# A transformer block on one core: the last second products go row tile by row tile, and a group's norm is spread over more tiles

## The chip, the cores and the metric

The kernel runs on one core of a Trainium2 chip. A core has engines that run beside each other, each through its own list of instructions in order: TensorE (PE in the profile; PEld is its loading of the stationary operand), VectorE (DVE), ScalarE (ACT) and GpSimd (POOL). SyncE (SP) issues the DMA transfers. An instruction that needs another engine's result waits on a semaphore, and everything behind it on its own engine waits with it. The metric is the time of one execution on the device, in microseconds (us); the median of several executions is compared.

## The reference

```python
h = _layernorm(x) * (1 + ca) + sa
x = x + ga * _A_ref(h, A_wqkv, A_wo)      # 16 heads, causal window of 256
h = _layernorm(x) * (1 + cb) + sb
x = x + gb * _B_ref(h, B_w1, B_b1, B_w2)

def _B_ref(x, w1, b1, w2):
    h = x @ w1 + b1
    act = h * tanh(softplus(h))            # Mish
    return act @ w2
```

There are 2048 rows of 448 float32 values; the feed-forward part `_B_ref` goes from 448 to 1792 columns and back. The six vectors sa, ca, ga, sb, cb, gb come from `silu(c) @ w_mod`. The change lies in the second half, the feed-forward part.

## The kernel before

**Precision.** Float32 products are made of two reduced-precision halves: a tensor is split into a high part and what is left, and a product is the sum of high by high, high by low and low by high. So `w13` and `w1l` are the two halves of the first weights, `w2h` and `w2l` those of the second, `hh` and `hl` those of the normalised input and `ah` and `al` those of the activation.

**Tiling.** The 2048 rows are four groups of 512 (`NG`, `GT`), and the 1792 hidden columns are 14 tiles of 128 (`NF`). The feed-forward part is one loop over n from 0 to 56 (`NN` is 56): n stands for group n // 14 and hidden tile n % 14. Attention fills the span up to about 370 us; the loop takes the rest.

**One step of the loop** (lines 1227 to 1246) issues, in this order:

- `f1_mm(n)`: the first product, 11 matmuls into one PSUM bank `z`. There are two such banks.
- `f1_act(n)`: ACT's Mish from `z` to `t`, ACT's copy to `ah`, and DVE's subtraction that gives `al` (lines 976 to 978). There are two buffers each of `ah` and `al`, one of `t`.
- `pieces(n)`, in the first group alone: the split of the weights that are still missing. Per tile this puts one copy `w2h` on ACT and one subtraction `w2l` on POOL.
- one `fill_step()`.
- `ff2(n - 1)`: the second product of the tile before, 12 matmuls: for each of the four row tiles t, three matmuls (`ah` by `w2h`, `ah` by `w2l`, `al` by `w2h`) into the bank `acc[g][t]`. On the last hidden tile of a group the row tile is finished: it is multiplied by `gbn` and the residual `x1` is added, in a buffer `yo` of which there are three (tag "xr"), and SP stores it.
- more `fill_step()`s: three in the first group, two in the others.

The order that is written here is the order on each engine; nothing rearranges it.

**What the fill steps do.** `fill` is a generator that hands out work beside the loop, a piece at each step. In the first group it first finishes the attention output of the last row group (`gen_oT`, `gen_wo`), and then makes the second group's normalised input: `gen_x1_ln2(1)`, which is `gen_ln2`. That is four DVE passes `xn` (one per row tile of 128), for which `XN2[g]` is set when they start, and then `ln2_blocks`: for each of four column chunks ci, 16 DVE transposes of 32x128 (four in one step, line 897), and then the two stages that `pipe` starts on its later steps: `hi(ci)`, which is ACT's `hhf` and behind it, in place, DVE's `yt` (lines 882 and 883), and `lo(ci)`, which is POOL's `hlf` (line 887). The third and fourth groups' inputs are made in the same way in groups 1 and 2, from their third tile on.

**The last group's finish.** For g = 3 the residual is added by POOL for row tiles 0 to 2, and for row tile 3 in two halves, 256 columns on DVE and 192 on POOL:

```python
for eng, a, b in (((DVE, 0, D),) if g < NG - 1 else ((POOL, 0, D),) if t < 3 else
                  ((DVE, 0, 256), (POOL, 256, D))):
    eng.tensor_tensor(y[:, a:b], y[:, a:b], x1[g][:, t, a:b], op=ALU.add)
```

Of the kernel before, what the change touches and what calls it, by code (L numbers as in the profile page):

```python
# [9 lines left out]
F32R = mybir.dt.float32r  # L10
BF16 = mybir.dt.bfloat16
AF = mybir.ActivationFunctionType
ALU = mybir.AluOpType

S, D, F, H, DH, W = 2048, 448, 1792, 16, 28, 256
NG, GT = 4, 512
# [35 lines left out]
def adaln_block(ctx: ExitStack, tc: tile.TileContext, x, wqkv, wo, w1, b1, w2, c, w_mod, out):  # L52
    nc = tc.nc
    PE, ACT, DVE, POOL = nc.tensor, nc.scalar, nc.vector, nc.gpsimd
# [3 lines left out]
    def dma(o, i):  # L58
        nc.sync.dma_start(o, i)

    def pool(name, side="left", space=None):
        kw = {} if space is None else {"space": space}
        cm = tc.tile_pool(name=name, bufs=1, reuse_waits="tile", side=side, **kw)
        st = ExitStack()
        return st.enter_context(cm), st
# [19 lines left out]
    def bank(tag, bufs, name):  # L85
        return PS[0].tile([128, 512], F32, name=name, tag=tag, bufs=bufs)
# [461 lines left out]
    def xr_tile(name):  # L548
        return mid.tile([128, 512], F32, name=name, tag="xr", bufs=3)
# [252 lines left out]
    FW = {}  # L802
    w2h, w2l, w2p, h2, x1 = {}, {}, {}, {}, {}
# [100 lines left out]
    XN2 = {}  # L904
# [37 lines left out]
    def pieces(f):  # L942
        for i, (kind, n) in enumerate(SEQ):
            if kind == "w2" and n == f:
                w2_split(n)
            elif kind == "w1" and (n - 4) // 2 == f:
                w1_hi(n)
                w1_lo(n, DVE if f < 1 else POOL)
            else:
                continue  # L950
            if "ff" in FW:
                piece_load(i + 6)

    NN = NG * NF
    ah, al, acc = {}, {}, {}

    def ftile(nm, n, dt=F32):
        return FW["p1"].tile([128, GT], dt, name=f"{nm}{n}", tag=nm, bufs=1 if nm == "t" else 2)
# [3 lines left out]
    def f1_mm(n, tag, part=(0, 11)):  # L962
        g, f = divmod(n, NF)
        hh, hl = h2[g]
        fs = slice(f * 128, (f + 1) * 128)
        if part[0] == 0:
            zb[n] = bank(tag, 2, f"z{n}")
        ps = passes(hh, hl, FW["w13"][:, :, fs], FW["w1l"][:, :, fs])
        for m in range(*part):
            PE.matmul(zb[n], ps[m][1], ps[m][0], start=(m == 0), stop=(m == 10))  # L970

    def f1_act(n):
        f = n % NF
        ah[n], al[n] = ftile("ah", n, F32R), ftile("al", n, F32R)
        t = ftile("t", n)
        ACT.activation(t, zb[n], AF.Mish, bias=FW["b1c"][:, f:f + 1])  # L976
        ACT.activation(ah[n], t, AF.Copy)  # L977
        DVE.tensor_tensor(al[n], t, ah[n].bitcast(F32), op=ALU.subtract)  # L978

    def mish_table():  # L980
# [4 lines left out]
    TAIL = {  # L985
        0: lambda: (f1_mm(0, "mm", (0, 6)), pieces(0)),
        1: lambda: (f1_mm(0, "mm", (6, 11)), mish_table(), f1_act(0)),
        2: lambda: f1_mm(1, "mm", (0, 6)),
        3: lambda: (f1_mm(1, "mm", (6, 11)), f1_act(1)),
    }  # L990

# [132 lines left out]
    for u in range(NU + 7):  # L1124
        s, k = divmod(u, 3)
        g = s // H
# [19 lines left out]
        if g < NG:  # L1146
# [6 lines left out]
            n = 0  # L1153
# [26 lines left out]
    ff, ff_s = pool("ff")  # L1180
    FW["ff"] = ff
    p1, gbn = FW["p1"], FW["gbn"]

    def ff2(n):
        g, f = divmod(n, NF)
        if f == 0:
            acc[g] = [bank("acc", 4, f"acc{g}_{t}") for t in range(4)]
        for t in range(4):
            ts = slice(t * 128, (t + 1) * 128)
            p = acc[g][t][:, 0:D]  # L1190
            PE.matmul(p, ah[n][:, ts], w2h[f], start=(f == 0), stop=False)  # L1191
            PE.matmul(p, ah[n][:, ts], w2l[f], start=False, stop=False)  # L1192
            PE.matmul(p, al[n][:, ts], w2h[f], start=False, stop=(f == NF - 1))  # L1193
            if f == NF - 1:
                j = 4 * g + t
                y = xr_tile(f"yo{j}")[:, 0:D]
                DVE.tensor_tensor(y, p, gbn, op=ALU.mult)
                for eng, a, b in (((DVE, 0, D),) if g < NG - 1 else ((POOL, 0, D),) if t < 3 else
                                  ((DVE, 0, 256), (POOL, 256, D))):
                    eng.tensor_tensor(y[:, a:b], y[:, a:b], x1[g][:, t, a:b], op=ALU.add)  # L1200
                dma(of[j * 128:(j + 1) * 128, :], y)

    def gen_x1_ln2(g):
        if g > 1:
            x1_load(g, (ff, p1)[g % 2])
            yield
            yield
            yield

        def xn_tiles():  # L1210
            t = XN2[g] = mid.tile([128, 4, 512], F32, name=f"xn2_{g}", tag="on", bufs=2)
            return [t[:, i] for i in range(4)]
        yield from gen_ln2(g, ff, xn_tiles, "tr", 2)
# [8 lines left out]
    def fill_step():  # L1222
        if fill is not None:
            pipe.step()
            next(fill, None)
            flush()
    for n in range(NN + 1):
        g, f = divmod(n, NF)
        if f == 0 and n:
            while fill is not None and next(fill, "END") != "END":  # L1230
                pipe.step()
            fill = None
            while pipe.items:
                pipe.step()
        if f == 2 and 0 < g < NG - 1:
            fill = gen_x1_ln2(g + 1)
        if 2 <= n < NN:
            f1_mm(n, "z")
            f1_act(n)
        if 0 < n < NF:  # L1240
            pieces(n)
        if n:
            fill_step()
            ff2(n - 1)
            for _ in range(2 + (g == 0)):
                fill_step()
    for st in (ff_s, mid_s, cst_s, FW["s"], psf_s):
        st.close()
# [23 lines left out]
```

## Time and profile before

| what | us |
|---|---|
| median of the 3 runs shown (661.86 to 669.27) | 663.73 |
| the profiled execution, its own time | 668.01 |
| its span, first to last instruction | 666.2 |
| the feed-forward loop within it, from the first second product on | 371.3 to 659.6 |

The profiled execution is 4.28 us above the median. The profile lists, for each engine, how long it was busy and what it waited for; in the timeline a row has the start, the duration, the engine, the source line and the tile, and in brackets how long the engine sat idle before it and which instruction ended that idle time. Matmuls overlap: a matmul is listed with 0.36 to 0.40 us, but one starts every 0.20 us (448 columns) or 0.23 us (512 columns) when nothing is missing.

### The profile page before, as it was taken

To read this page: it belongs to the slowest core of one execution; us is meant where nothing else is said; L and a number is where in the kernel's file an instruction comes from. 1 tells how busy PE (TensorE), PEld (TensorE's weight loads), DVE (VectorE), ACT (ScalarE), POOL (GpSimd) and SP (SyncE) were. 2 spreads that over 40 slices of the span, in tenths; PEclk is the share of its full clock that TensorE was granted. 3 is DMA by queue.
4 is the path that set the end of the run, shared out by engine and by line. 5 is a ranking of instruction groups with operands and counts; after the bars stand their busy time and mean duration, and the time that the engine had idled before them with its cause. 6 is when DMAs were issued, how large, how long until landed. Compare 5 with 4: busy or idle time off the path is not lost.

```text
span 666.2 us, 10727 instructions
## 1 busy us (share of the span) xinstructions
PE 634.8 (95%) x3712; PEld 514.3 (77%) x3712; DVE 391.1 (59%) x1138; ACT 335.6 (50%) x584; POOL 120.6 (18%) x173
## 2 busy tenths in 40 slices
PE   3998999999999999999988999999999999999996
PEld 3786777677887678877756898878888888888885
DVE  5765686675678767578777334954584438631112
ACT  4544567588875778635668633432233224323221
POOL 6652000043011200000030445340021001100002
PEclk9997999599999999999999999999999999999999
DMA  8786676547754478435852853003000300010001
GB/s 215 211 233 215 225 245 213 147 114 227 270 172 142 141 224 307 147 110 151 235 150 69 261 148 106 11 1 111 0 1 0 112 1 0 1 55 1 1 0 55
DMA packets 49169, 83.77 MB, mean 126 GB/s; under 512 B 5838, under 2 KB 27612, under 8 KB 49116
## 3 DMA queue, kind: packets, MB, share of 16 engines
q1 hardware_dynamic: 49116, 83.10, 40.6%
q8 instruction: 29, 0.48, 0.3%
q14 instruction: 24, 0.20, 0.1%
HBM read 53.45 MB, written 29.36 MB: 124 GB/s over the span
## 4 chain that ended last, share of the span: by engine, by line
PE 74%; issue 11%; DVE 8%; DMA 3%; ACT 2%; SPq 1%; POOL 1%; POOLq 0%; DVEq 0%; ACTq 0%
PE z L970 15%; PE qk L321 10%; PE pv L769 7%; PE sA L687 6%; PE sB L731 6%; PE wo L321 5%; PE acc L1193 4%; PE acc L1191 4%; PE acc L1192 4%; PE qk_v L321 4%; DVE yt L897 3%; DMA k<-scr 2%; PE sB L759 2%; DVE junk L689 1%; PE qk L506 1%
## 5 line engine op out<-in xcount | busy, mean ns | idle before, releaser
L689 DVE CUSTOM_DVE_ANT_0 junk<-sA,strip 128x384 bf16<-128x384 f32 (+2 forms) x256 | 135.4, 529 | 80.6 <-PE sA L687 65.8
L734 ACT ACTIVATE P<-sB 128x512 f32<-128x512 f32 (+2 forms) x192 | 108.3, 570 | 84.5 <-PE sB L731 82.1
L978 DVE TENSOR_TENSOR al<-t,ah 128x512 fp32r<-128x512 f32 x56 | 41.2, 735 | 137.2 <-ACT ah L977 136.9
L976 ACT ACTIVATE t<-z,b1c 128x512 f32<-128x512 f32 x56 | 38.4, 686 | 156.8 <-PE z L970 145.0
L970 PE MATMUL z<-hhf,w 128*128 128x512 f32 x224 | 88.9, 397 | 0.0
L970 PE MATMUL z<-hlf,w 128*128 128x512 f32 x224 | 88.8, 397 | 0.0
L731 PE MATMUL sB<-q,k 86*128 86x384 f32 (+1 forms) x352 | 87.2, 323 | 0.7 <-ACT sB L739 0.7
L687 PE MATMUL sA<-k,q 84*128 84x384 f32 (+2 forms) x256 | 82.4, 360 | 4.3 <-DMA k<-scr 2.7
L1193 PE MATMUL acc<-w2h,al 128*128 128x448 f32 x224 | 82.1, 366 | 1.9 <-DVE al L978 1.9
L1191 PE MATMUL acc<-w2h,ah 128*128 128x448 f32 x224 | 81.9, 366 | 0.0
L1192 PE MATMUL acc<-w2l,ah 128*128 128x448 f32 x224 | 81.8, 365 | 0.0
L731 PEld LDWEIGHTS sB<-q,k 86*128 86x128 f32 x352 | 60.3, 197 | 11.1 <-ACT sB L739 4.4
L970 PE MATMUL z<-hhf,w1l 128*128 128x512 f32 x168 | 66.5, 396 | 0.0
L897 DVE STREAM_TRANSPOSE yt<-xn 32x128 f32<-32x128 f32 x192 | 58.1, 302 | 2.6
L687 PEld LDWEIGHTS sA<-k,q 84*128 84x128 f32 x256 | 48.4, 197 | 10.4 <-DVE mx L689 2.7
L739 ACT ACTIVATE sB<-strip 128x512 f32<-128x512 bf16 (+2 forms) x95 | 54.6, 575 | 3.0
L769 PE MATMUL pv<-P,v 128*32 128x256 f32 (+2 forms) x704 | 50.2, 399 | 0.4 <-DVE on L790 0.4
L970 PEld LDWEIGHTS z<-hlf,w 128*128 128x128 f32 x224 | 42.1, 188 | 10.1
L970 PEld LDWEIGHTS z<-hhf,w 128*128 128x128 f32 x224 | 42.1, 188 | 9.1 <-issue 0.6
L1193 PEld LDWEIGHTS acc<-w2h,al 128*128 128x128 f32 x224 | 42.1, 188 | 5.9 <-DVE al L978 2.6
L1191 PEld LDWEIGHTS acc<-w2h,ah 128*128 128x128 f32 x224 | 42.1, 188 | 5.0
L1192 PEld LDWEIGHTS acc<-w2l,ah 128*128 128x128 f32 x224 | 42.1, 188 | 4.7
(155 smaller groups left out, 1029.1 us busy)
## 6 DMA issues: line engine op xcount, KB each, us to landing
k<-scr SPq DMA_DIRECT2D x48, 252.0 KB
q<-scr SPq DMA_DIRECT2D x64, 168.0 KB
scr<-st SPq DMA_DIRECT2D x21, 512.0 KB
scr<-st SPq DMA_DIRECT2D x29, 256.0 KB
x<-x1d SPq DMA_DIRECT2D x10, 448.0 KB
xin<-in_A_x_dram SPq DMA_DIRECT2D x8, 448.0 KB
xr<-in_A_x_dram SPq DMA_DIRECT2D x16, 224.0 KB
x1d<-xr SPq DMA_DIRECT2D x16, 224.0 KB
```

Of the source, the lines that this page charges most:

```text
L321: PE.matmul(p, b, a, start=(n == 0), stop=(n == 10))
L687: PE.matmul(p[:, c0:384], q[0:84, t * 128:(t + 1) * 128], k[0:84, t * 128 + c0:t * 128 + 384], start=True, stop=True)
L689: DVE.tensor_tensor_reduce(out=junk[:, c0:384], in0=p[:, c0:384], in1=mask[:, c0:384], scale=1.0, scalar=-3.0e38, op0=ALU.add, op1=ALU.max ...
L731: PE.matmul(p[:, c:c + 128 * (t1 - t0)], k[:, jj * 128:(jj + 1) * 128], q[:, t0 * 128:t1 * 128], start=False, stop=True, skip_group_check= ...
L734: ACT.activation(P[:, c0:], p[:, c0:], AF.Exp, scale=SCALE)
L739: ACT.activation(p[:, c0:], strip[:, c + c0:c + 512], AF.Copy)
L769: PE.matmul(pvb[q][32 * a:32 * a + 32, t0 * 128:t1 * 128], V[j % NV][:, h + a, :], Pt[4 * w + a][:, c:c + 128 * (t1 - t0)], start=(b == 0 ...
L897: DVE.transpose(y4[32 * j:32 * j + 32, ci, :, 32 * i:32 * i + 32], x4[32 * i:32 * i + 32, :, ci, 32 * j:32 * j + 32])
L970: PE.matmul(zb[n], ps[m][1], ps[m][0], start=(m == 0), stop=(m == 10))
L1191: PE.matmul(p, ah[n][:, ts], w2h[f], start=(f == 0), stop=False)
L1192: PE.matmul(p, ah[n][:, ts], w2l[f], start=False, stop=False)
L1193: PE.matmul(p, al[n][:, ts], w2h[f], start=False, stop=(f == NF - 1))
```

## The change

Three things change, in the functions `f1_act` and `ff2` and in the loop.

1. The second products of the last three tiles (n = 53, 54, 55) are no longer issued a step behind their first products. They all go to the end, behind the first product of tile 55: first row tiles 0 and 1 of tile 53; then, for each row tile in turn, what it still lacks (54 and 55 for row tiles 0 and 1; 53, 54 and 55 for 2 and 3). Since three activations are then alive at once, tile 55 gets buffers for `ah` and `al` of its own, from the pool that the weights were staged in.
2. In the last group the residual is added by DVE alone, for all four row tiles, in one piece, as in the other groups.
3. In the first group, the fill steps behind `ff2` are no longer always three: two at n up to 4, four from n = 5 until the second group's norm has started (`1 in XN2`), and two from there on. With the one ahead of `ff2` this makes three, five and three in a step in place of four.

```diff
     def f1_act(n):
         f = n % NF
-        ah[n], al[n] = ftile("ah", n, F32R), ftile("al", n, F32R)
+        if n == NN - 1:
+            ah[n], al[n] = (FW["ff"].tile([128, GT], F32R, name=f"{x}{n}", tag="stg", bufs=6) for x in ("ah", "al"))
+        else:
+            ah[n], al[n] = ftile("ah", n, F32R), ftile("al", n, F32R)
...
-    def ff2(n):
+    def ff2(n, tiles=range(4)):
...
-        for t in range(4):
+        for t in tiles:
...
                 DVE.tensor_tensor(y, p, gbn, op=ALU.mult)
-                for eng, a, b in (((DVE, 0, D),) if g < NG - 1 else ((POOL, 0, D),) if t < 3 else
-                                  ((DVE, 0, 256), (POOL, 256, D))):
-                    eng.tensor_tensor(y[:, a:b], y[:, a:b], x1[g][:, t, a:b], op=ALU.add)
+                DVE.tensor_tensor(y, y, x1[g][:, t, :D], op=ALU.add)
                 dma(of[j * 128:(j + 1) * 128, :], y)
...
             fill_step()
-            ff2(n - 1)
-            for _ in range(2 + (g == 0)):
+            if n == NN:
+                ff2(n - 3, (0, 1))
+                for t in range(4):
+                    for last in range(n - 3 + (t < 2), n):
+                        ff2(last, (t,))
+            elif n < NN - 2:
+                ff2(n - 1)
+            for _ in range(2 + (g == 0 and 1 not in XN2) * (1 + (n > 4))):
                 fill_step()
```

The counts on each engine stay as they were but for the adds: DVE has four of 448 columns in place of one of 256, and POOL's four are gone. How the instructions stand in the row is shown at three places. In each row are the source line, the operation, and what it writes and reads, with the tile's number n behind `al`, `ah`, `z` and the output row tile's behind `yo`.

DVE in the first group, from the second group's `xn` passes to the last piece of its norm, before:

```order
L244 TENSOR_SCALAR xn2_1_5046<-x1_1_4726,mv2_1_402,rsf1_5043 128x448
L978 TENSOR_TENSOR al6_5061<-t6_5062,ah6_5060 128x512
L244 TENSOR_SCALAR xn2_1_5046<-x1_1_4726,mv2_1_402,rsf1_5043 128x448 x3
...
L978 TENSOR_TENSOR al8_5159<-t8_5160,ah8_5158 128x512
L883 TENSOR_SCALAR yt1_5117<-yt1_5117,cols_182 128x512
L897 STREAM_TRANSPOSE yt1_5117<-xn2_1_5046 32x4x32 x16
L978 TENSOR_TENSOR al9_5212<-t9_5213,ah9_5211 128x512
...
L978 TENSOR_TENSOR al11_5318<-t11_5319,ah11_5317 128x512
L883 TENSOR_SCALAR yt1_5117<-yt1_5117,cols_182 128x512
L978 TENSOR_TENSOR al12_5355<-t12_5356,ah12_5354 128x512
```

and after:

```order
L244 TENSOR_SCALAR xn2_1_5046<-x1_1_4726,mv2_1_402,rsf1_5043 128x448 x2
L981 TENSOR_TENSOR al6_5063<-t6_5064,ah6_5062 128x512
...
L981 TENSOR_TENSOR al8_5155<-t8_5156,ah8_5154 128x512
L897 STREAM_TRANSPOSE yt1_5117<-xn2_1_5046 32x4x32 x4
L883 TENSOR_SCALAR yt1_5117<-yt1_5117,cols_182 128x512
L897 STREAM_TRANSPOSE yt1_5117<-xn2_1_5046 32x4x32 x8
L981 TENSOR_TENSOR al9_5204<-t9_5205,ah9_5203 128x512
...
L981 TENSOR_TENSOR al12_5348<-t12_5349,ah12_5347 128x512
L897 STREAM_TRANSPOSE yt1_5117<-xn2_1_5046 32x4x32 x4
L883 TENSOR_SCALAR yt1_5117<-yt1_5117,cols_182 128x512
L981 TENSOR_TENSOR al13_5389<-t13_5390,ah13_5388 128x512
```

Between two `al` there were 16 transposes and are now 12; the 64 transposes begin behind `al7` as before and end behind `al12` in place of ahead of `al11`, and one `xn` pass more stands ahead of `al6`.

PE at the end of the program, before: behind the first product of tile 55 (its last row is the first here) come all four row tiles of tile 54 and then of tile 55.

```order
L970 MATMUL z55_6888<-hlf3_6148,w13_3996 128x512
L1191 MATMUL acc3_0_6542<-w2h12_5360,ah54_6870 128x448
...
L1193 MATMUL acc3_3_6545<-w2h12_5360,al54_6871 128x448
L1191 MATMUL acc3_0_6542<-w2h13_5394,ah55_6900 128x448
L1192 MATMUL acc3_0_6542<-w2l13_5395,ah55_6900 128x448
L1193 MATMUL acc3_0_6542<-w2h13_5394,al55_6901 128x448
```

and after:

```order
L970 MATMUL z55_6876<-hlf3_6148,w13_3996 128x512
L1194 MATMUL acc3_0_6542<-w2h11_5304,ah53_6840 128x448
...
L1196 MATMUL acc3_1_6543<-w2h11_5304,al53_6841 128x448
L1194 MATMUL acc3_0_6542<-w2h12_5353,ah54_6870 128x448
L1195 MATMUL acc3_0_6542<-w2l12_5354,ah54_6870 128x448
L1196 MATMUL acc3_0_6542<-w2h12_5353,al54_6871 128x448
L1194 MATMUL acc3_0_6542<-w2h13_5394,ah55_6888 128x448
L1195 MATMUL acc3_0_6542<-w2l13_5395,ah55_6888 128x448
L1196 MATMUL acc3_0_6542<-w2h13_5394,al55_6889 128x448
```

So 11 matmuls, no longer 14, stand between the end of `z55` and the first one that reads `al55`, and the four row tiles are finished 6, 9 and 9 matmuls apart in place of 3.

DVE at the end of the program, before:

```order
L1197 TENSOR_TENSOR yo12_6921<-acc3_0_6542,gbn_4616 128x448
L1197 TENSOR_TENSOR yo13_6928<-acc3_1_6543,gbn_4616 128x448
L1197 TENSOR_TENSOR yo14_6935<-acc3_2_6544,gbn_4616 128x448
L1197 TENSOR_TENSOR yo15_6942<-acc3_3_6545,gbn_4616 128x448
L1200 TENSOR_TENSOR yo15_6942<-yo15_6942,x1_3_6042 128x256
```

and after, the last two row tiles, each product followed by its add:

```order
L1200 TENSOR_TENSOR yo14_6929<-acc3_2_6544,gbn_4616 128x448
L1201 TENSOR_TENSOR yo14_6929<-yo14_6929,x1_3_6042 128x448
L1200 TENSOR_TENSOR yo15_6942<-acc3_3_6545,gbn_4616 128x448
L1201 TENSOR_TENSOR yo15_6942<-yo15_6942,x1_3_6042 128x448
```

POOL has no instruction left behind the last `hlf`.

## The prediction

> **What bounds the kernel now.** I read the page first, to see which engine carries the span, and in it the groups for what that engine waits for.
>
> ```profile
> PE 634.8 (95%) x3712; PEld 514.3 (77%) x3712; DVE 391.1 (59%) x1138; ACT 335.6 (50%) x584; POOL 120.6 (18%) x173
> PEclk9997999599999999999999999999999999999999
> L1193 PE MATMUL acc<-w2h,al 128*128 128x448 f32 x224 | 82.1, 366 | 1.9 <-DVE al L978 1.9
> ```
>
> PE is busy for 95% of the span, and the change neither removes nor adds a matmul. So it can give back only what PE loses by waiting, and what comes behind its last matmul. Of the waits the group of L1193, the matmul that reads `al`, is the only one in the feed-forward loop, and it waits for DVE. Next I asked for the engines' busy time in two stretches of the first group, and for PE's timeline there.
>
> ```profile
> 428.00:438.00 10.00, 9.23 (x42) 7.57 (x41) 9.45 (x30) 3.32 (x6) 4.27 (x4) 1.00 0.01 2
> 438.00:448.00 10.00, 8.90 (x41) 7.44 (x40) 3.75 (x7) 4.36 (x7) 4.49 (x5) 1.00 0.00 1
> ```
>
> The columns are the stretch, its length, then PE, PEld, DVE, ACT and POOL busy, the granted clock, the share of DMA and GB/s. PE has holes in both, DVE is at 9.45 of 10 in the first, and the clock stays at 1.00.
>
> ```profile
> 431.74 0.37 PE L1191 MATMUL acc<-w2h,ah 128*128 128x448 f32 x1
> 433.08 0.47 PE L1193 MATMUL acc<-w2h,al 128*128 128x448 f32 x1 [0.77 <-DVE al L978]
> 437.80 0.37 PE L1191 MATMUL acc<-w2h,ah 128*128 128x448 f32 x1
> 439.47 0.47 PE L1193 MATMUL acc<-w2h,al 128*128 128x448 f32 x1 [1.10 <-DVE al L978]
> 444.18 0.37 PE L1191 MATMUL acc<-w2h,ah 128*128 128x448 f32 x1
> ```
>
> The L1191 rows are the first matmuls of three second products in a row (n = 10, 11, 12). They are 6.06 and 6.38 us apart. The period without a wait is 5.00 (from the ACT rows below), so PE loses 1.06 + 1.38 = 2.4 us there. DVE shows why:
>
> ```profile
> 427.26 5.04 DVE L897 STREAM_TRANSPOSE yt<-xn 32x128 f32<-32x128 f32 x16
> 432.33 0.69 DVE L978 TENSOR_TENSOR al<-t,ah 128x512 fp32r<-128x512 f32 x1
> 433.19 0.55 DVE L883 TENSOR_SCALAR yt<-yt,cols 128x512 f32<-128x512 f32 x1 [0.16 <-ACT hhf L882]
> 433.65 5.04 DVE L897 STREAM_TRANSPOSE yt<-xn 32x128 f32<-32x128 f32 x16
> ```
>
> One round of `al`, `yt` and 16 transposes takes 433.65 - 427.26 = 6.39 us, 1.39 more than PE's period. Over the four rounds DVE falls 5.6 us behind. The first 3.1 or so are slack: `al` is finished 2.1 us after its Mish starts (654.75 to 656.82) and read 5.2 us after (649.73 to 654.96, rows below). The rest is PE's loss.
>
> The other loss is behind the last matmul. I read it from the timeline of the last 12 us and from the rows of tile `yo`:
>
> ```profile
> 649.73 0.69 ACT L976 ACTIVATE t<-z,b1c 128x512 f32<-128x512 f32 x1 [3.66 <-PE z L970]
> 654.55 0.37 PE L1191 MATMUL acc<-w2h,ah 128*128 128x448 f32 x1
> 654.75 0.69 ACT L976 ACTIVATE t<-z,b1c 128x512 f32<-128x512 f32 x1 [3.66 <-PE z L970]
> 654.96 0.36 PE L1193 MATMUL acc<-w2h,al 128*128 128x448 f32 x1
> 656.13 0.69 DVE L978 TENSOR_TENSOR al<-t,ah 128x512 fp32r<-128x512 f32 x1 [4.32 <-ACT ah L977]
> 656.98 0.36 PE L1191 MATMUL acc<-w2h,ah 128*128 128x448 f32 x1
> 657.79 1.85 DVE L1197 TENSOR_TENSOR yo<-acc,gbn 128x448 f32<-128x448 f32 x3 [0.97 <-PE acc L1193]
> 658.50 3.31 POOL L1200 TENSOR_TENSOR yo<-yo,x 128x448 f32<-128x448 f32 x3 [81.25 <-DVE yo L1197]
> 659.23 0.36 PE L1193 MATMUL acc<-w2h,al 128*128 128x448 f32 x1
> 659.67 3.95 SPq L59 DMA_DIRECT2D out_dram<-yo  x4
> 661.73 0.62 DVE L1197 TENSOR_TENSOR yo<-acc,gbn 128x448 f32<-128x448 f32 x1 [2.08 <-DMA out_dram<-yo]
> 662.43 0.83 POOL L1200 TENSOR_TENSOR yo<-yo,x 128x192 f32<-128x192 f32 x1 [0.62 <-DVE yo L1197]
> L59 SPq DMA_DIRECT2D out_dram<-yo x4: 332/332/332, 659.7 to 663.3; - x4
> ```
>
> PE ends at 659.59. The last row tile's product on DVE starts only at 661.73, because its buffer is that of the first of the four and the store out of that buffer was issued at 659.67: 2.06 us to land. Then come the product, POOL's half of the add (0.83) and the last store, issued at 659.67 + 3.95 - 0.33 = 663.29. The span ends 2.9 us later, at 666.2.
>
> **The change, step by step.**
>
> *The norm spread over more tiles (first group).* Nothing is added or removed. With 12 transposes to a tile (0.315 each, 5.04 / 16) a round without `yt` is 0.69 + 3.78 = 4.5 us and one with it 5.0, against the period of 5.00. But behind four transposes `yt` stands without an `al` between, and DVE then waits for ACT's `hhf`. What that costs, the second group shows, where the same order has been running all along (it has three fill steps to a tile already):
>
> ```profile
> 484.51 0.69 ACT L976 ACTIVATE t<-z,b1c 128x512 f32<-128x512 f32 x1 [0.85 <-PE z L970]
> 509.50 0.69 ACT L976 ACTIVATE t<-z,b1c 128x512 f32<-128x512 f32 x1 [3.17 <-PE z L970]
> 487.42 2.52 DVE L897 STREAM_TRANSPOSE yt<-xn 32x128 f32<-32x128 f32 x8
> 490.82 0.55 DVE L883 TENSOR_SCALAR yt<-yt,cols 128x512 f32<-128x512 f32 x1 [0.89 <-ACT hhf L882]
> 492.56 0.73 DVE L978 TENSOR_TENSOR al<-t,ah 128x512 fp32r<-128x512 f32 x1
> 505.12 0.55 DVE L883 TENSOR_SCALAR yt<-yt,cols 128x512 f32<-128x512 f32 x1 [0.88 <-ACT hhf L882]
> ```
>
> The two Mish rows are five tiles apart: 24.99 / 5 = 5.00 us, so PE lost nothing while this pattern ran. How near was it? `al` is read 654.96 - 649.73 = 5.2 us after its Mish falls due. The latest one (492.56, ended 493.29) belongs to the Mish due at 484.51 + 5.00 = 489.51, so it was wanted at 494.7: 1.4 us to spare. In the first group ACT also has `w2h` and POOL also has `w2l`, and one `xn` pass more stands ahead of `al6`. I take the wait to be gone, since the nearest row shows 1.4 us spare: 2.4 us less. The ends: 2.4 is all there is to gain. At the other end, each `al` that falls beside `w2l` can take as long as the longest in the trace:
>
> ```profile
> 418.98 1.51 DVE L978 TENSOR_TENSOR al<-t,ah 128x512 fp32r<-128x512 f32 x1
> 428.19 0.56 ACT L939 ACTIVATE w2h<-w2p 128x448 fp32r<-128x448 f32 x1
> ```
>
> That is 0.82 more for six tiles, 4.9 us, and `w2h` could put 0.56 ahead of each of four `hhf`, 2.2 more. All of it in series would be 7.1 us of lag, and after the 1.4 spare 5.7 us of wait, 3.3 more than now. It is not all in series, since DVE also idles before most `al`.
>
> *Second products at the end.* PE's 36 matmuls of the last three tiles stay 36, 0.20 us apart ((656.98 - 654.55) / 12). What covers the chain of `z55` gets shorter. `al55` ends at 656.82, 2.27 us behind the first matmul after `z55` (654.55). Its matmul stood 14 places behind and now stands 11 behind: 2.23 us, and its weights are loaded one place sooner. So PE waits a little. After the wait at 433.08 the matmul that followed began 0.37 us after `al` had ended (433.39 against 433.02), so here at 2.27 + 0.37 = 2.64 where 2.43 was its turn: 0.2 us more, with 0 and 0.4 as ends. Tiles 53 and 54 are long finished by then. `ah55` has new buffers and waits for nobody; the `z` bank that `z55` takes was read by the Mish of tile 53, a whole tile earlier.
>
> *Adds on DVE.* DVE idles at the end, and its adds lie between row tiles 6 to 9 matmuls (1.2 to 1.8 us) apart. What product and add take, the end of the first group shows:
>
> ```profile
> 451.39 0.62 DVE L1197 TENSOR_TENSOR yo<-acc,gbn 128x448 f32<-128x448 f32 x1
> 452.70 0.34 SPq L59 DMA_DIRECT2D out_dram<-yo  x1
> ```
>
> From the product to the store's issue it is 1.31 us, product, add and semaphores. The last row tile's own product no longer waits for its buffer: 24 matmuls, 4.9 us, lie between the first row tile's end and its own, and the store is done 1.31 + 2.06 = 3.4 us after that first end. So PE ends at 659.59 + 0.2, DVE starts 0.04 later as at 657.79, and the last store is issued at 659.83 + 1.31 = 661.14 in place of 663.29: 2.15 us less. Ends: 1.9 to 2.4, by the wait for `al55`. POOL's four adds go and nobody waits for POOL. The 2.9 us behind the issue stay, since the last store already ran alone.
>
> *Sum.* 2.4 + 2.15 = 4.55 us less, 0.7%. Against the profiled execution that is 668.01 to 663.5; it stood 4.28 above the median, so on the median's footing 663.73 - 4.55 = **659.2 us**.
>
> **Rivals.**
>
> 1. *Part of the wait in the first group stays* because the spare of 1.4 us is used up by `w2h` and `w2l`. Half of it left gives 2.4 / 2 + 2.15 = 3.35: 660.4. All of it left gives 661.6. For it: the 1.51 us of one `al`. Against it: 1.4 us free in the same order.
> 2. *The tail does not shorten as said*: the last store still waits, on a buffer or on DVE. At worst only the first group's 2.4 is gained: 661.3. Against it: 1.5 us spare at the buffer.
> 3. *Slower: the second group's input comes too late.* The last `hlf` moves behind `al12`. In the second group the same `yt` ends at 505.67, 6.2 us after the Mish due at 484.51 + 15 = 499.5; POOL's `hlf` adds about 1.3. Two tiles later, PE reads that chunk 9.3 us after the same point (two periods less the 11 matmuls of 0.23 and 0.2, plus nine of them): 1.8 us spare. Each us of DVE's lag beyond 1.8 holds PE at the start of the second group. It outweighs both gains from 1.8 + 4.55 = 6.3 us of lag on; at the 7.1 of the upper end above it would be 0.8 us slower, 664.5.
> 4. *The stalls also cost clock*, and without them the clock rises. If each had held PE at the 5 tenths of the page's lowest slice for one period of 5.00, 2 x 2.5 us more would be won: 654.2. The two stretches show 1.00 throughout, so I give this almost nothing. [...]
> 5. *The clock's early dips differ.* The page's PEclk row has two slices at 7 and 5 tenths in the first 150 us, which the change does not touch. The runs shown spread over 7.4 us. A median of few runs can so lie 4 us to either side: 655 or 663.
>
> **The numbers.** A change under 1%, 6.6 us, is about what a measurement of this kernel can't tell from none. My forecast has 0.66, rival 1 0.13, rival 2 0.07, rival 3 0.03, rival 4 0.02, rival 5 0.09, half to each side. The range from 655.5 to 663.0 takes in rivals 1 and 2 and nearly all of 5. Faster by over 1% (below 657.1) needs rival 4, the low side of 5, or the forecast with a low median: 0.13. Slower by over 1% (above 670.4) no term reaches; it is left 0.02 for disturbed medians. Within 1%: 0.85.
>
> **What the profile afterwards would show.** Right: no wait of L1196 for `al` between 425 and 445, second products 5.0 us apart through the whole first group, 12 transposes between two `al`, last store issued about 1.6 us behind PE's last end, no wait for a store ahead of the last `yo`. Wrong: PE waiting for `hlf` at the first product of n = 14, for `al` in some tile from 6 to 12, or over 0.4 us for `al55`.

## The result

Over 20 runs of each kernel the changed one took 661.46 us at the median (657.73 to 665.3) and the kernel before 667.23 (661.44 to 669.76). The ratio over all these runs is 0.9934, with a 95% interval of 0.9912 to 0.9956: 0.66% faster, or 4.4 us of 667 (2.9 to 5.9). (The two medians by themselves stand at 0.9914, inside that interval.) That is within 1%, as forecast, with the time inside the range. The predicted 659.2 is 2.3 us low: the 3 runs of before on which it stood had a median 3.5 us below that of the 20.

The profiled execution has a span of 659.0 us against 666.2. These 7.2 us are not all the change. The page of the changed kernel begins the comparison:

```profile
PE 629.2 (95%) x3712; PEld 509.7 (77%) x3712; DVE 393.9 (60%) x1141; ACT 335.4 (51%) x584; POOL 117.0 (18%) x169
PEclk9999999899999999999989999999999999999999
L1195 PE MATMUL acc<-w2l,ah 128*128 128x448 f32 x224 | 81.9, 366 | 0.4 <-POOL w2l L940 0.4
```

The early dips of the clock are shallower in this execution (no slice under 8 tenths, against 7 and 5; a mean of 0.99 over the first 150 us against 0.93), and the feed-forward loop starts earlier: its first second product begins at 368.00 against 371.34. That code is the same in both kernels, and 3.34 of the 7.2 us are chance: a second profile of the changed kernel has that matmul at 366.53. So I measure from that first matmul on:

```
from the first second product, us     before    after    difference
to the end of PE's last matmul        288.25    286.73     1.52
to the issue of the last store        291.95    288.08     3.87
to the end of the span                294.9     291.0      3.9
```

3.9 us come from the change, where the prediction summed 4.55; they lie well inside the interval of the timing.

In the first group, the two stretches that correspond to those shown of before (4 us earlier, as the loop starts 3.34 us earlier; columns as there):

```profile
424.00:434.00 10.00, 9.62 (x45) 7.97 (x44) 8.61 (x26) 5.10 (x8) 4.62 (x4) 1.00 0.01 2
434.00:444.00 10.00, 10.00 (x48) 8.62 (x47) 6.76 (x17) 4.28 (x7) 5.12 (x6) 1.00 0.00 1
```

PE is full in the second and has one hole in the first. PE's timeline has that hole at the second product of n = 10, and it is not `al` that ends it:

```profile
428.45 0.37 PE L1194 MATMUL acc<-w2h,ah 128*128 128x448 f32 x1
429.20 0.47 PE L1195 MATMUL acc<-w2l,ah 128*128 128x448 f32 x1 [0.38 <-POOL w2l L940]
434.12 0.37 PE L1194 MATMUL acc<-w2h,ah 128*128 128x448 f32 x1
```

434.12 - 428.45 = 5.67 us against a period of 5.01 elsewhere. The two periods of before, 6.06 and 6.38, are gone; 0.66 us are new.

At the end of the program, the timeline and the stores of tile `yo`:

```profile
649.38 0.19 PEld L1196 LDWEIGHTS acc<-w2h,al 128*128 128x128 f32 x1 [0.31 <-DVE al L981]
654.37 0.36 PE L1196 MATMUL acc<-w2h,al 128*128 128x448 f32 x1
654.76 0.62 DVE L1200 TENSOR_TENSOR yo<-acc,gbn 128x448 f32<-128x448 f32 x1 [0.55 <-PE acc L1196]
655.42 0.63 DVE L1201 TENSOR_TENSOR yo<-yo,x 128x448 f32<-128x448 f32 x1
L59 SPq DMA_DIRECT2D out_dram<-yo x4: 332/332/333, 651.2 to 656.1; - x4
```

The load that waits for `al55` is 0.31 us late. The last row tile's product waits for PE alone and starts 0.03 us behind the end of the last matmul; the last store goes out 1.35 us behind it, where it was 3.70.

### The profile page after: what moved, and what is told of

Same layout as the page of the kernel before. It is cut to its first block, busy times and chain, and to the rows that moved or that the text cites. A ratio compares the mean times of both kernels' runs of the same rounds, so it can differ in the third digit from the quotient of the medians.

```text
span 659.0 us, 10719 instructions
## 1 busy us (share of the span) xinstructions
PE 629.2 (95%) x3712; PEld 509.7 (77%) x3712; DVE 393.9 (60%) x1141; ACT 335.4 (51%) x584; POOL 117.0 (18%) x169
## 4 chain that ended last, share of the span: by engine, by line
PE 86%; DVE 5%; DMA 2%; ACT 2%; issue 2%; POOL 1%; SPq 1%; DVEq 0%; POOLq 0%; ACTq 0%
PE z L970 21%; PE qk L321 9%; PE pv L769 7%; PE acc L1196 7%; PE acc L1195 7%; PE acc L1194 6%; PE sA L687 6%; PE sB L731 6%; PE wo L321 5%; PE qk_v L321 4%; PE sB L759 2%; DVE junk L689 2%; DMA k<-scr 2%; PE qk L506 1%; PE mt L705 1%
## 5 line engine op out<-in xcount | busy, mean ns | idle before, releaser
L731 PE MATMUL sB<-q,k 86*128 86x384 f32 (+1 forms) x352 | 85.2, 316 | 0.7 <-ACT sB L739 0.7
L687 PE MATMUL sA<-k,q 84*128 84x384 f32 (+2 forms) x256 | 80.7, 353 | 3.6 <-DMA k<-scr 1.9
L731 PEld LDWEIGHTS sB<-q,k 86*128 86x128 f32 x352 | 58.7, 193 | 11.1 <-ACT sB L739 4.4
L687 PEld LDWEIGHTS sA<-k,q 84*128 84x128 f32 x256 | 46.9, 190 | 9.9 <-DVE mx L689 2.9
L970 PEld LDWEIGHTS z<-hlf,w 128*128 128x128 f32 x224 | 42.1, 188 | 10.1
```

What stands on the lines that cost most here:

```text
L687: PE.matmul(p[:, c0:384], q[0:84, t * 128:(t + 1) * 128], k[0:84, t * 128 + c0:t * 128 + 384], start=True, stop=True)
L731: PE.matmul(p[:, c:c + 128 * (t1 - t0)], k[:, jj * 128:(jj + 1) * 128], q[:, t0 * 128:t1 * 128], start=False, stop=True, skip_group_check= ...
```

## The experiments

All are measured from the first second product, since that time repeats. In 13 profiled executions the first second product began anywhere from 365.85 to 372.73 (with a mean granted clock of 0.997 over the span in the first of these two, the ninth experiment's, and 0.981 in the other, the tenth's), but the four kernels that leave the order of the matmuls and the norm as they were (before, and the third, fifth and sixth below) then need 288.25, 288.24, 288.24 and 288.24 us to PE's last end.

### The norm alone

```diff
-            for _ in range(2 + (g == 0)):
+            for _ in range(2 + (g == 0 and 1 not in XN2) * (1 + (n > 4))):
```

> The kernel before with the fill steps of the first group alone changed. Measured from the first second product, so that the clock's early dips stay out: in the kernel before it is 288.25 us to the end of PE's last matmul and 291.95 us to the issue of the last store. Theory (the gain in the first group is PE's 2.4 us of waiting for al, of which a new wait for w2l at n = 10 gives back 0.65): 286.5 and 290.2, the wait for w2l of about 0.4 us is there, none for al. Rival (the wait for w2l comes from the part at the end, or is chance): 285.85 and 289.55 and no wait for w2l.

Measured: 286.49 us to PE's last end and 290.19 to the last store. All of PE's waits from the first second product on (line, releaser, us in total, times, longest):

```profile
PE acc L1192 <- POOL w2l L940: 0.4, 1, 0.4
```

The theory holds to 0.01 us. This part gains 1.76 us; it takes away both waits for `al` and brings the wait for `w2l` with it.

### The end alone

```diff
-            for _ in range(2 + (g == 0 and 1 not in XN2) * (1 + (n > 4))):
+            for _ in range(2 + (g == 0)):
```

> The changed kernel with the three fill steps of before in the first group, so only the end is changed. From the first second product. Theory (the end gains 2.15 us behind PE's last matmul and loses 0.2 us to the wait for al55): 288.45 us to PE's last end, 289.8 to the issue of the last store, both waits for al at n = 10 and 11 as before. Rival (the two parts act on each other, and the end alone gains more or less): the issue of the last store more than 0.3 us off 289.8.

Measured: 288.46 us to PE's last end and 289.80 to the last store, with PE's and PEld's waits

```profile
PE acc L1196 <- DVE al L981: 1.9, 2, 1.1
PEld acc L1196 <- DVE al L981: 2.9, 3, 1.5
```

PE's two waits are those of before, and the third of PEld is that for `al55`. This part gains 2.15 us and costs PE 0.21. The two parts add up: 1.76 + 2.15 = 3.91 against 3.87 together.

### DVE's adds alone

```diff
-                for eng, a, b in (((DVE, 0, D),) if g < NG - 1 else ((POOL, 0, D),) if t < 3 else
-                                  ((DVE, 0, 256), (POOL, 256, D))):
-                    eng.tensor_tensor(y[:, a:b], y[:, a:b], x1[g][:, t, a:b], op=ALU.add)
+                DVE.tensor_tensor(y, y, x1[g][:, t, :D], op=ALU.add)
```

> The kernel before with all four adds of the last group on DVE, the order of the matmuls as it was. Theory (the buffer of the first row tile still holds the last one, only its store goes out sooner): store of the first row tile 1.31 us behind its product, 2.06 us to land, product of the last row tile at about 1.6 us behind PE's last end, last store issued 2.9 us behind PE's last end in place of 3.7. Rival (POOL was what held the end, and its adds on DVE give all of the gain): 1.35 us.

Measured: last store 3.10 us behind PE's last end (656.98), a gain of 0.6. DVE's timeline there, the last four rows:

```profile
657.58 0.62 DVE L1197 TENSOR_TENSOR yo<-acc,gbn 128x448 f32<-128x448 f32 x1
658.23 0.63 DVE L1198 TENSOR_TENSOR yo<-yo,x 128x448 f32<-128x448 f32 x1
658.77 0.62 DVE L1197 TENSOR_TENSOR yo<-acc,gbn 128x448 f32<-128x448 f32 x1
659.43 0.62 DVE L1198 TENSOR_TENSOR yo<-yo,x 128x448 f32<-128x448 f32 x1
```

The rival falls, and my theory in part: the last product started 1.79 us behind PE's end, and no idle time stands ahead of it, so not the buffer held it but DVE itself. (The store out of its buffer was issued at 656.49; with the 2.06 us of before it was done at about 658.55, ahead of the product's start at 658.77.) A product and an add take 1.19 us, and the row tiles came 0.6 us apart.

### The order alone

The new order of the matmuls with POOL's adds: the changed kernel with the line of the end-alone experiment and the lines of the adds, just above, put back as they were before.

> The kernel before with the new order of the last three tiles' second products, but the adds as they were: on POOL, and the last one halved between DVE and POOL. Theory (the new spacing of the row tiles takes the buffer off the path, POOL's part only adds the difference between its halved add and DVE's whole one): last store issued 0.04 + 1.56 = 1.6 us behind PE's last end, against 1.35 with DVE's adds and 3.7 before. Rival (without DVE's adds the stores go out too late and the buffer still holds the last row tile): over 2 us.

Measured: last store 1.65 us behind PE's last end; PE's end is at 288.44. So the order is what counts: of the 2.35 us by which the last store draws nearer to PE's end, it gives 2.05, and DVE's adds on top of it 0.3. POOL's timeline, its last two rows:

```profile
656.51 1.15 POOL L1203 TENSOR_TENSOR yo<-yo,x 128x448 f32<-128x448 f32 x1 [0.68 <-DVE yo L1200]
658.40 0.83 POOL L1203 TENSOR_TENSOR yo<-yo,x 128x192 f32<-128x192 f32 x1 [0.74 <-DVE yo L1200]
```

It idles ahead of both, so it has no queue any more.

### A buffer of its own for the last row tile

```diff
-                y = xr_tile(f"yo{j}")[:, 0:D]
+                y = (xr_tile(f"yo{j}") if j < 15 else FW["ff"].tile([128, 512], F32, name="yo15", tag="stg", bufs=6))[:, 0:D]
```

> The kernel before with a buffer of its own for the last row tile, nothing else. Theory (the wait for the store of 2.1 us is only the last of two things, POOL's queue of adds is the next): product of the last row tile right behind PE's last end, its add on POOL after the three others, last store issued 3.1 us behind PE's last end in place of 3.7, so 0.6 of the 2.1 us. Rival (the buffer is all of it): 1.6 us.

Measured: 2.99 us behind PE's last end in place of 3.70. The wait of 2.08 us for the store is gone, yet only 0.7 is won:

```profile
657.35 2.46 DVE L1197 TENSOR_TENSOR yo<-acc,gbn 128x448 f32<-128x448 f32 x4 [0.96 <-PE acc L1193]
658.05 4.06 POOL L1200 TENSOR_TENSOR yo<-yo,x 128x448 f32<-128x448 f32 x4 [81.25 <-DVE yo L1197]
```

All four products follow one another on DVE without a wait, and POOL's four adds, 4.06 us without a gap, are the next limit.

### Both: the buffer and DVE's adds, in the old order

The two edits above together.

> The kernel before with the adds of the last group on DVE and a buffer of its own for the last row tile, the order of the matmuls as it was. With the adds alone the last store was issued 3.10 us behind PE's last end. Theory (with row tiles three matmuls apart, 0.6 us, DVE's product and add of 1.19 us each queue on DVE itself, and the buffer no longer counts): 3.10 again. Rival (the store of the first row tile still held the buffer): 2.9 or less.

Measured: 3.10 us, as the theory had it. With row tiles three matmuls apart, a buffer and a faster add do not add up, since DVE's own queue is the floor.

### The norm spread thinner still

```diff
-            for _ in range(2 + (g == 0 and 1 not in XN2) * (1 + (n > 4))):
+            for _ in range(2 - (g == 0 and 1 in XN2) + (g == 0 and 1 not in XN2) * (1 + (n > 4))):
```

> The changed kernel with one fill step fewer per tile in the first group once the norm has started: two, so 8 transposes between two al in place of 12. It asks where spreading ends. Theory (the second group's input must be there at n = 14; 64 transposes at 8 a tile need eight tiles, of which seven are there, the rest is then issued at once): no wait for al or w2l in the first group, but PE waits at the first products of n = 14 for hlf, 2 to 5 us, and the end of PE's last matmul is later than in the changed kernel by as much. Rival (DVE has so much room that the last pieces come in time): no wait at n = 14, and 0.65 us less than the changed kernel, whose wait for w2l goes.

Measured: 296.13 us to PE's last end, 9.4 more than the changed kernel. The first group has no wait for `al` or `w2l`, but PE waits at the first product of n = 14, as the theory said; PE's timeline has these four waits:

```profile
441.58 0.50 PE L970 MATMUL z<-hhf,w 128*128 128x512 f32 x1 [0.47 <-ACT hhf L882]
443.50 0.49 PE L970 MATMUL z<-hlf,w 128*128 128x512 f32 x1 [1.19 <-POOL hlf L887]
447.95 0.79 PE L970 MATMUL z<-hhf,w 128*128 128x512 f32 x1 [3.96 <-ACT hhf L882]
449.88 0.80 PE L970 MATMUL z<-hlf,w 128*128 128x512 f32 x1 [1.13 <-POOL hlf L887]
```

The waits sum to 6.75 us, above the 2 to 5 I expected, since the last 16 transposes all came (442.02 to 447.05) when PE already stood there. And the loss is more than their sum: the matmuls listed with 0.79 and 0.80 us are of kinds that took 0.39 and 0.40 in the same run where the granted clock was 1.00. The busy times in four stretches of that place, with the granted clock as the third figure from the end:

```profile
440.00:444.00 4.00, 2.34 (x8) 1.05 (x6) 3.01 (x11) 0.81 (x1) 1.66 (x2) 1.00 0.00 0
444.00:446.00 2.00, 0.00 (x0) 0.00 (x0) 1.92 (x7) 0.00 (x0) 0.00 (x0) 0.52 0.00 0
452.00:454.00 2.00, 2.00 (x7) 1.79 (x6) 1.82 (x4) 0.12 (x1) 0.00 (x0) 0.50 0.00 0
454.00:456.00 2.00, 2.00 (x10) 1.70 (x9) 1.93 (x5) 0.00 (x0) 0.00 (x0) 0.92 0.31 115
```

The clock is at a half from about 444 to 454 (0.50 in each stretch of 2 us from 446 to 454). So this is where spreading ends: 12 transposes to a tile are in time, 8 are not.

### The weights' split ahead of Mish

```diff
             f1_mm(n, "z")
-            f1_act(n)
         if 0 < n < NF:
             pieces(n)
+        if 2 <= n < NN:
+            f1_act(n)
```

> The changed kernel with pieces(n) issued ahead of f1_act(n): on ACT the copy w2h of a tile stands ahead of its Mish in place of behind its ah. Measured from the first second product: in the changed kernel 286.73 us to the end of PE's last matmul. Theory (w2h at n = 10 was late because it stood behind a Mish that stood behind hhf, and w2l on POOL behind it): w2h and w2l are 1.3 us earlier there, the wait for w2l goes, 286.1 us. Rival (w2l is late for another reason, POOL being shared or its length): the wait stays, 286.7. Second rival (Mish now stands 0.56 us later in every tile and al takes the wait over): a wait for al of 0.3 us or more and 286.7 or above.

Measured: 286.27 us, 0.46 less than the changed kernel. The period at n = 10 is 5.01, so the theory's wait is gone. But the period at n = 13 is now 5.24. POOL's timeline shows why:

```profile
443.64 1.30 POOL L887 TENSOR_TENSOR hlf<-yt,hhf 128x512 fp32r<-128x512 f32 x1 [4.72 <-DVE yt L883]
444.89 1.60 POOL L940 TENSOR_TENSOR w2l<-w2p,w2h 128x448 fp32r<-128x448 f32 x1
```

The last `w2l` stands behind the last `hlf` and ends at 446.49; the matmul that reads it started at 446.55, 0.33 behind the one ahead of it in place of 0.20.

### More cover for the last activation

```diff
-                ff2(n - 3, (0, 1))
+                ff2(n - 3, (0, 1, 2))
                 for t in range(4):
-                    for last in range(n - 3 + (t < 2), n):
+                    for last in range(n - 3 + (t < 3), n):
```

> The changed kernel with row tiles 0, 1 and 2 of tile 53 ahead of the row-tile order in place of 0 and 1: three matmuls more between the first product of tile 55 and the first matmul that reads al55. Measured from the first second product: in the changed kernel 286.73 us to PE's last end. Theory (the wait for al55, 0.3 us on the loads, costs 0.2 us): no wait for al55, 286.5 us, last store 1.35 us behind PE's last end. Rival (loads of weights run ahead enough that the wait costs nothing): 286.73 us.

Measured: 286.50 us, 0.23 less; no wait for `al55` is left, and the last store still goes out 1.35 us behind PE's end. So the wait of 0.31 us on the load cost 0.2 on PE, as worked out.

### Both waits taken away

```diff
-        if 0 < n < NF:
-            pieces(n)
+        for m in (n,) if n < 6 else (6, 7) if n == 6 else (n + 1,):
+            if 0 < m < NF:
+                pieces(m)
...
-                ff2(n - 3, (0, 1))
+                ff2(n - 3, (0, 1, 2))
...
-                    for last in range(n - 3 + (t < 2), n):
+                    for last in range(n - 3 + (t < 3), n):
```

> The changed kernel with two edits: from tile 6 on the split of the second weights is issued a tile earlier, and three row tiles of tile 53 stand ahead of the row-tile order. Measured from the first second product; the changed kernel has 286.73 us to PE's last end and 288.08 to the issue of the last store. Theory (what PE still lost were 0.66 us of waiting for w2l at n = 10 and 0.2 for al55): no wait on PE for w2l or al, every period of the first group from n = 4 on 5.0 us, 285.85 and 287.2 us. Against the kernel before 4.75 us less, a ratio of about 0.993. Rival (the earlier split puts POOL or ACT in the way of hlf, al or Mish at another tile): another period longer than 5.1 us and 286.3 or more.

Measured: 285.88 us to PE's last end and 287.22 to the last store. From n = 4 on no period of the first group is above 5.04. PE has no wait at all in the loop; one load waits 0.2 us without holding a matmul:

```profile
PEld acc L1195 <- POOL w2l L940: 0.2, 1, 0.2
```

In time it took 660.21 us at the median of 12 runs (657.22 to 665.95), a ratio of 0.9934 to the kernel before (0.9895 to 0.9973).

### The changed kernel again

> The changed kernel once more, on the same chip as the version with w2l a tile earlier, so that the two can be set side by side. Both theories: 286.73 us from the first second product to PE's last end as before, ratio to the kernel before 0.993 to 0.994; the times of the two are not told apart, since 0.9 us is under what the clock's early dips move.

Measured: 286.72 and 288.07 us; 662.18 at the median of 12 runs (659.72 to 665.0), a ratio of 0.994 (0.9909 to 0.997). From the first second product to the last store the version with both waits taken away is 0.85 us shorter. Their times are not told apart, as the intervals overlap almost wholly. The version is better by the profile, and that is all that is shown.

The periods of the second products of n = 7 to 13 (start of one to the start of the next) set the runs of the first group side by side:

```
                         7     8     9     10    11    12    13
before                  5.02  5.02  5.01  6.06  6.38  5.02  5.01
changed                 5.02  5.02  5.01  5.67  5.01  5.01  5.02
weights ahead of Mish   5.02  5.02  5.01  5.01  5.01  5.02  5.24
both waits taken away   5.03  5.01  5.01  5.02  5.01  5.01  5.02
spread thinner          5.03  5.01  5.01  5.02  5.01 13.36  6.76
```

(The 13.36 holds the first product of n = 14, which is issued between the second products of n = 12 and n = 13.)

## Why the prediction was right, and where it was not

- **DVE held PE for 2.4 us in the first group, and the spreading would end that.** Right. Both waits for `al` are gone when the norm alone is changed, and the 12, 4 and 8, 8 and 4 transposes between two `al` run as in the second group.
- **The gain there is the whole 2.4 us.** Wrong in size: 1.76. I took the spare from the second group, where the order has no `w2h` and `w2l`, gave their part only as a bound, and costed it on `al` alone. What came late was `w2l` itself. The rows of the changed kernel, from DVE, POOL and ACT, show the chain that led to it:

```profile
420.58 1.15 POOL L940 TENSOR_TENSOR w2l<-w2p,w2h 128x448 fp32r<-128x448 f32 x1 [0.74 <-ACT w2h L939]
420.85 1.42 DVE L981 TENSOR_TENSOR al<-t,ah 128x512 fp32r<-128x512 f32 x1
422.31 2.52 DVE L897 STREAM_TRANSPOSE yt<-xn 32x128 f32<-32x128 f32 x8
424.86 0.82 ACT L882 ACTIVATE hhf<-yt,cols 128x512 fp32r<-128x512 f32 x1 [4.36 <-DVE yt L897]
425.58 0.67 ACT L979 ACTIVATE t<-z,b1c 128x512 f32<-128x512 f32 x1
426.82 0.56 ACT L939 ACTIVATE w2h<-w2p 128x448 fp32r<-128x448 f32 x1
427.45 0.69 DVE L981 TENSOR_TENSOR al<-t,ah 128x512 fp32r<-128x512 f32 x1
427.46 1.68 POOL L940 TENSOR_TENSOR w2l<-w2p,w2h 128x448 fp32r<-128x448 f32 x1 [5.74 <-ACT w2h L939]
```

  `al9` starts beside `w2l9` and takes 1.42 us in place of 0.69. So the 8 transposes behind it, and `hhf`, are late. ACT is idle for 4.36 us ahead of that `hhf`, but works in order: Mish of n = 10 stands behind it, and `w2h` behind Mish. Then `w2l10` in turn starts beside `al10` and takes 1.68 in place of 1.15. It ends at 429.14, and PE had wanted it 0.2 us behind 428.45. Putting `w2h` ahead of Mish, or a tile earlier, takes the wait at n = 10 away; that the doubled `al9` alone would have been enough to cause it was not tried.
- **Rival 1, part of the wait stays because of `w2h` and `w2l`,** had that place and cause, on another operand. It had 0.13, and about a quarter of the gain went its way. The prediction's sign of second products 5.0 us apart through the whole first group failed at n = 10.
- **The wait for `al55` costs 0.2 us.** Right: 0.21 with the end alone, and 0.23 won back with more cover.
- **The last store is issued 1.35 us behind PE's last end in place of 3.70, and the 2.9 us behind it stay.** Right: 1.35, and the span ends 2.9 us later in both. (The prediction's list of signs says about 1.6; its own sum, 661.14 against PE's end at 659.79, is 1.35.)
- **What held the end.** The prediction named the buffer. The runs show three limits one behind the other, all near 3 us: the store's 2.06 us in the buffer (3.70), POOL's four adds (2.99 without the buffer's wait) and DVE's products and adds (3.10 with both taken away). Of what was tried, only row tiles that are finished further apart remove all three; the order gives 2.05 of the 2.35 us, and the adds the rest.
- **Rival 2, the tail does not shorten as said,** did not happen: the end alone gains the 2.15 us. In the changed kernel the store out of the last row tile's buffer is issued at 651.20 and the product begins at 654.76, so with 2.06 us to land the buffer was free 1.5 us ahead, as summed.
- **Rival 3, the second group's input too late,** did not happen, but in the thin run PE did wait for that input, 6.75 us at n = 14. The prediction gave 1.8 us of spare. In the changed kernel the last `hlf` ends at 442.02, and the matmul of n = 14 that reads it starts at 443.91: 1.9 us. (That matmul is the last of the eleven, so ten stand ahead of it; the prediction counted nine.)
- **Rival 4, the stalls cost clock,** did not happen here: waits of 0.77 and 1.10 us, 6.4 us apart, left the clock at 1.00 in the kernel before. In the thin run the clock did fall where PE had stalled: to half at about 444.1, by estimate, since a share of 0.52 over 444 to 446 leaves 0.08 us at full speed. The matmul listed at 443.50 had ended at 443.99, so the wait of 3.96 us had only begun; what lay close ahead of the fall were the waits of 0.47 and 1.19 us. Whether their length, their nearness or something else counts was not tried. The share of 0.92 over 454 to 456 puts the return to full, by estimate, at 454.3, 4.4 us behind the start of the matmul at 449.88, from which on PE ran without a wait.
- **Rival 5, the clock's early dips differ,** came in part, in its effect: the median of 3 runs on which the forecast stood was 3.5 us low (no clock of those runs is known, so that the dips made it so is not shown). From the median of the 20, 667.23, the sum of 4.55 gives 662.7, near the upper end of the range, and the changed kernel's median came 1.2 us below that. So it is partly luck that the time lies only 2.3 us from the forecast, and it is the stretch from the first second product that bears the mechanism out. A change under 1% could be told from none here: with 20 runs of each the interval of the ratio ends at 0.9956.

## What to carry to other kernels

Compare kernels over the stretch that the change can touch: here it repeats within 0.02 us, while its start moves by 6.9 us, from 365.85 at a mean granted clock of 0.997 to 372.73 at 0.981. When a queue is shortened by moving work, ask of each engine what stands in order behind the moved pieces: it was not the operand that had been late that came late afterwards, but the next one behind it on ACT and POOL. And at the end of a program, before adding buffers or engines to the finish, look whether the pieces can be finished further apart, so that each one's finish lies under the next one's matmuls.

## What the runs showed of the hardware

- **Of an `al` on DVE and a subtraction (`w2l`, `hlf`) on POOL that overlapped, the one that started later ended last, by nearly the same time in each case.** In the changed kernel's loop seven `al` started behind POOL's and ended 0.54 to 0.55 us behind its end, and nine `w2l` started behind `al` and ended 1.00 to 1.03 us behind its end. So `al`, 0.69 us at the median of 56, took 1.42 when it started 0.27 us behind `w2l9` (`al9` lay beside it for 0.88 us and ended 0.54 behind it), and `w2l` took 1.15 as the earlier one (`w2l9`) and 1.68 when it started 0.01 us behind `al10`. What holds the later one up, no run shows.
- **In the thin run PE's waits came with a fallen clock, and the loss was more than the waits.** It lost 9.4 us against the changed kernel although it saved 0.66 at n = 10; its waits at n = 14 are 6.75 of these 10.1. Most of the other 3.3 falls where the granted clock was 0.50: PE was busy for 5.2 us between 447.95 and 454.3, by estimate 2.6 us more than at full clock.
